# A transformer layer on one core: the order of jobs and values, transfers one by one, and layernorm roots by a power

## The chip, the core and the metric

The kernel runs on one core of one Trainium2 chip. A core has five engines with instruction streams of their own: TensorE (PE in the profile, its weight loads PEld), VectorE (DVE), ScalarE (ACT), GpSimd (POOL) and SyncE (SP), which issues nearly all transfers here. They share the on-chip memory SBUF; TensorE writes its products to PSUM, a second memory of 8 banks per partition, from which VectorE and ScalarE read them. Each engine works through its instructions in the order in which the program has them, and waits at semaphores for the others.

The metric is the device time of one execution in microseconds; lower is better.

## The reference

One pre-norm transformer layer, with a sequence of 2048, width 640, 32 heads of 20 and a hidden width of 1728. All inputs are bfloat16.

```python
def _A_ref(x, wqkv, wo):                      # B, S, D = 1, 2048, 640; H = 32; Dh = 20
    qkv = (x @ wqkv).reshape(B, S, 3, H, Dh).transpose(2, 0, 3, 1, 4)
    q, k, v = qkv[0], qkv[1], qkv[2]
    scores = jnp.einsum("bhqd,bhkd->bhqk", q, k) * (Dh ** -0.5)
    p = _softmax(scores, axis=-1)
    o = jnp.einsum("bhqk,bhkd->bhqd", p, v)
    return o.transpose(0, 2, 1, 3).reshape(B, S, D) @ wo
def _B_ref(x, w_gate, w_up, w_down):          # F = 1728
    g = jnp.einsum("bsd,df->bsf", x, w_gate)
    u = jnp.einsum("bsd,df->bsf", x, w_up)
    return jnp.einsum("bsf,fd->bsd", g * u, w_down)
h = x + _A_ref(_layernorm(x), wqkv, wo)       # _layernorm: (x - mean) / sqrt(var + 1e-5)
h2 = h + _B_ref(_layernorm(h), w_gate, w_up, w_down)
```

The softmax is over 32 x 2048 x 2048 scores, 134 million exponentials.

## The kernel before

**Tiling.** The heads are in 8 groups of 4; each head has a slot of 32 partitions, so four heads' scores or values run side by side in TensorE's array. Queries are in four blocks of 512 rows (b = 0 to 3), keys in 16 tiles of 128. A segment is one group's attention for one block (for the later blocks, of most groups, a half block of 256). All segments, one after the other, are cut into 683 score tiles of 1536 columns (three PSUM banks, two tiles in PSUM at a time).

**The main loop** runs over these tiles. `emit_S` issues a tile's scores (L533) and its exponential on ScalarE (L547), which writes bfloat16 into one of six buffers E. For some tiles the last 512 columns are left to VectorE, which makes the exponential of them with four instructions (L580 to L591): then ScalarE's tile has only 1024 columns. `x_takes` decides this by how much VectorE has to do and by how many such slices (tile xe) are still waiting to be used (`X_OUT`, 6). `emit_AV` takes the exponentials of finished tiles, two rounds of four heads at a time, and multiplies them with the values (L740); the extra column of ones in the values makes the softmax's sums. At a segment's end the accumulator is copied to SBUF (tile asb, L752); the sums go to DRAM and back over SP, are inverted on VectorE, broadcast by further transfers, and multiplied with asb some tiles later (`norm`).

**Jobs.** All other work of TensorE is in a queue of jobs, generators that yield one matmul (or one transposed tile) at a time: projections of queries, keys (L303) and values (L317), transposes of normalised rows (L283), the output projection (`job_out`, L978), the feed-forward's up and gate products (`job_glu`, L1065; with half blocks `glu_two`, L1083) and its second layer (`job_y`, L1129, 14 matmuls for half a row tile). Nearly all share one PSUM bank (tile mi): a job's result has to be evacuated by VectorE before the next job can begin. Where there is no job that fits, and TensorE's clock might fall, filler matmuls are issued (L496, L529).

**The planner.** The order on each engine is made while the program is built. The dictionary `at` holds estimated times: when TensorE, VectorE and ScalarE are done with what has been issued, when the bank mi is free (`at["mi"]`), when a score tile's slot is free. After a tile's scores and the values, `run_job(until)` issues pieces of jobs as long as they end, by the estimate, before the next scores have to be begun: `until` is the later of two times, the end of ScalarE's exponentials less 517 ns, and the moment at which the slot of the tile before the last is free. `spare` fills VectorE in the same way with layernorm steps and exponential slices. `later(n, fn)` calls a function n tiles further on.

**Layernorms.** Means and variances are made by VectorE (L201, L202). `rstd_steps` then rounds them to bfloat16 as the reference does, and makes the standard deviation on GpSimd with a shift of bits (L218), three Newton rounds of four instructions (L221 to L225) and a product (L232). At the earliest `ROOT_NS` (5000 ns) later, by the planner's clock, VectorE takes the reciprocal (L238) and normalises the rows. There are ten of these in the program's main part: three for the first layernorm (the first block's is made with ScalarE), seven for the second.

**Transfers.** When block 0's attention is finished, `add_tail` queues its output projection and feed-forward; its job `ready` asks for the rows of x, the first two pairs of up and gate weights (`load_w`) and all 14 tiles of the second-layer weights (`load_wd`, L956). When block 0's feed-forward is through, eight jobs `spill` copy the queries to DRAM (L935, L936), for a second pass that runs only if a sum is out of range; the freed SBUF then takes feed-forward weights for good (`load_res`). Other up and gate weights have two buffers each, and the next pair is asked for when a step begins (L1036).

**The end.** Behind the loop `last_tail` handles the last 256 rows: it issues the output projection (L1228, L1230, L1234), with the last group's normalisation in between (L670, L686), then statistics, ScalarE's root, and the normalised rows in halves on VectorE (L1257) and ScalarE (L1258). `fill()` issues all jobs that are left while these are made. Then come two tiles' transposes, the feed-forward, and the second layer with stores.

```python
            for f in range(2 * FP):
                p0 = max(0, (f + 1) * P - FF)
...
        for _ in range(2):
            emit_AV(i if i >= n_tiles else i - 2 if i >= LAG else i - 3)
...
            ran = run_job(max(at["exp"] - S_EXP - MARGIN, at["slot"][-2]))
...
        while cur["fresh"] or pe_free("F") + chunk() + SWITCH <= until:
            c = step()
            if c == FREE and cur["key"][0] not in ("spill", "load"):
```

Of the kernel before, what the change touches and what calls it, by code (L numbers as in the profile page):

```python
# [19 lines left out]
P = 128  # L20
# [40 lines left out]
RES_STEPS = 3  # L61
WO_NS, SUMS_NS, ROOT_NS, ROWS_NS = 1500, 6000, 5000, 5000
END_OF_TIME = 10 ** 9
WARM_LATE, NEXT_DVE = 0, 300
HOLD_AT, HOLD_NS = 5300, 450
AV_ROUNDS, X_LATE = 2, 0
FULL_IN, FULL_NS, ALL_NS = 2083, 300, 760
X_LEAST, X_OUT, X_SOON = 2, 6, 4
# [17 lines left out]
def kernel(  # L86
# [42 lines left out]
    huge = const.tile([P, 1], F32, name="huge")  # L129
    wo = [const.tile([P, D], BF16, name=f"wo{g}") for g in range(NG)]  # L130
# [52 lines left out]
    nc.gpsimd.memset(huge[:], 3.0e38)  # L183
    for c in range(KT):
        nc.vector.memset(wpad[c][:].rearrange("p m h e -> p (m h) e")[:, :, DH:SLOT], 0.0)
# [18 lines left out]
    def rstd_steps(mv, n, made, ve_=None):  # L204
        ve_ = ve_ or nc.vector
        mb = small.tile([P, n], BF16, name="mb")
        ve_.tensor_copy(mb[:], mv[:, :, 0])  # L207
# [7 lines left out]
        ve_.tensor_copy(v[:], ve[:])  # L215
        yield 1000 if ve_ is nc.vector else 50
        y = small.tile([P, n], F32, name="y")
        ve_.tensor_scalar(y[:].bitcast(I32), v[:].bitcast(I32), -0.5, float(0x5F3759DF), ALU.mult, ALU.add)  # L218
        t = small.tile([P, n], F32, name="nt")
        for k in range(3):  # L220
            ve_.tensor_tensor(t[:], y[:], y[:], ALU.mult)  # L221
            if ve_ is nc.gpsimd:
                ve_.tensor_tensor(t[:], t[:], v[:], ALU.mult)
                ve_.tensor_scalar(t[:], t[:], -0.5, 1.5, ALU.mult, ALU.add)
                ve_.tensor_tensor(y[:], t[:], y[:], ALU.mult)  # L225
            else:
                ve_.scalar_tensor_tensor(t[:], t[:], -0.5, v[:], ALU.mult, ALU.mult)
                ve_.scalar_tensor_tensor(y[:], t[:], 1.5, y[:], ALU.add, ALU.mult)
            if k != 2:
                yield (800, 600)[k] if ve_ is nc.vector else 50  # L230
        den = small.tile([P, n], BF16, name="den")
        ve_.tensor_tensor(den[:], v[:], y[:], ALU.mult)  # L232
# [5 lines left out]
        nc.vector.reciprocal(r[:], den[:])  # L238
        made.append((m32, r))
        yield 1000 if ve_ is nc.vector else 200  # L240
# [260 lines left out]
    def run_job(until):  # L501
# [9 lines left out]
        while cur["fresh"] or pe_free("F") + chunk() + SWITCH <= until:  # L511
            c = step()
            if c == FREE and cur["key"][0] not in ("spill", "load"):
                return run_job(until)
            if c in (None, NEXT, END, FREE):
                break
# [189 lines left out]

    def emit_AV(upto):
# [40 lines left out]
        if acc["left"] == 0:  # L748
            dve(605 if w == QB else 342, 0)
            if kind in ("copy", "only"):  # L750
                asb = parts[g] if kind == "copy" else nrm.tile([P, QB], F32, name="asb")
# [182 lines left out]
    def spill(g):  # L934
        nc.sync.dma_start(qsp[g][:, 0:QA], qa[g][:])  # L935
        nc.sync.dma_start(qsp[g][:, QA:S], qb[g][:])  # L936
# [14 lines left out]
    def load_wd():  # L951
        for f in range(2 * FP):
            p0 = max(0, (f + 1) * P - FF)
            if p0:
                nc.gpsimd.memset(late["Wd"][f][0:p0, :], 0.0)
            nc.sync.dma_start(late["Wd"][f][p0:P, :], B_w_down[f * P:f * P + P - p0, :])  # L956
# [120 lines left out]
    def glu_two(st, fp, c0, n):  # L1077
        u = late["s"].tile([P, QB], BF16, name="u")
        for k in range(2):
            ps = bank()  # L1080
            for f2 in range(2):
                for c in range(KT):
# [9 lines left out]
                    yield 216 * n // QB  # L1092
            yield NEXT
# [6 lines left out]
    def job_glu(st, ts, order=tuple(range(FP)), more=False):  # L1100
# [4 lines left out]
        for k, fp in enumerate(order):  # L1105
# [5 lines left out]
            if n <= HW and end["pool"] is None:  # L1111
                yield from glu_two(st, fp, c0, n)
# [52 lines left out]
    def add_tail(b, ts):  # L1165
        key = (b, ts[0])

        def ready():
            if key not in rows_in:
                rows(b, ts)  # L1170
            if b == 0:
                load_w(0, tail_st[b])
                load_w(1, tail_st[b])
                load_wd()
# [22 lines left out]
        if b == 0:  # L1197
            for g in range(NG):
                do(("spill", g), lambda g=g: spill(g))
# [18 lines left out]
    def last_tail():  # L1218
# [36 lines left out]
        for hf in range(2):  # L1255
            cs = slice(hf * HALF, (hf + 1) * HALF)
            nc.vector.tensor_scalar(ls[ta][:, cs], ps_h[ta, hf][:, 0:HALF], m32[:, 0:1], r[:, 0:1], ALU.subtract, ALU.mult)  # L1257
            nc.scalar.activation(ls[tb][:, cs], ps_h[tb, hf][:, 0:HALF], ACT.Identity, bias=mr[:, 1:2], scale=r[:, 1:2])  # L1258
        fill()
        run(job_T(ls[ta], st["ln2T"][:, :, ta * P:(ta + 1) * P], "dve", mip.tile([P, D], BF16, name="mi", tag="mi")))  # L1260
# [49 lines left out]
    while i < n_tiles or av_q:  # L1310
# [6 lines left out]
        if i == first_last:  # L1317
            for g in range(NG):
                ensure(("spill", g))
# [37 lines left out]
    def general():  # L1357
        st = new_st(None)
        st["res"] = {}
        with tc.For_i(0, S, P) as r0:  # L1360
# [3 lines left out]
            for g in range(NG):  # L1364
# [37 lines left out]
                oq = nrm.tile([P, HPG, SLOT], BF16, name="oq", tag="asb")  # L1402
# [41 lines left out]
```

## Time and profile before

| | |
|---|---|
| median of 3 runs | 916.38 us (915.68 to 917.12) |
| the profiled execution | 916.05 us, of which the span on the core is 914.0 us |
| granted TensorE clock, mean | 0.997 |
| score tiles on ScalarE | 515 of 1536 columns, 168 of 1024 columns |
| exponential slices on VectorE | 167 of 512 columns |
| first exponential begins, last one ends | 15.6 us, 869.9 us |
| transfers | 46.54 MB, mean 51 GB/s |

How to read the lines: the page begins with each engine's busy time, its share of the span and its number of instructions. A group's row names the line, the engine, the operation, the tile written and the tiles read, the shapes, the count, then the busy time in us and the mean of one in ns, and the idle time of the engine just before them with what ended it. A row of the timeline begins with its start and its length in us and ends in brackets with idle time before it and what ended that. A row of a table by stretches begins with the stretch in us from the span's start and its length. A row of the waits says who waited for whom, the us in total, the number of times, and the longest.

### The profile page before, as it was taken

How to read it: one execution, taken by the hardware profiler on the slowest of the kernel's cores; microseconds unless marked ns; L12 is line 12 of the kernel's file. 1: busy time of each engine (PE TensorE's matmuls, PEld its weight loads, DVE VectorE, ACT ScalarE, POOL GpSimd, SP SyncE). 2: the span in 40 equal slices, each digit the busy share in tenths (PEclk: the TensorE clock that was granted, in tenths of full speed). 3: DMA queues.
4: the chain of work that ended last, by engine and by line, in shares of the span. 5: the costliest groups of instructions: out<-in, count | busy, mean ns of one | idle time of the engine just before them, and what ended most of it. 6: DMA issues, size and time to landing. Idle time of an engine off the chain costs nothing.

```text
span 914.0 us, 20094 instructions
## 1 busy us (share of the span) xinstructions
PE 817.5 (89%) x8035; PEld 346.8 (38%) x8115; DVE 702.1 (77%) x1310; ACT 866.2 (95%) x719; POOL 57.4 (6%) x255
## 2 busy tenths in 40 slices
PE   8788999889989899899897888999998999998897
PEld 5233333222223222233232333434434445444575
DVE  8664349899999899899998999798998784542243
ACT  6999999999999999999999999999999999999931
POOL 4210000000001200000003000020001000010000
PEclk9999999999999999999999999999999999999999
DMA  6000011011025022212410022021411211201310
GB/s 195 17 14 1 1 27 27 14 24 37 4 61 149 13 71 72 64 49 90 160 28 14 20 70 68 19 54 49 117 51 42 73 28 51 57 15 50 80 44 18
DMA packets 74203, 46.54 MB, mean 51 GB/s; under 512 B 20380, under 2 KB 70440, under 8 KB 74104
## 3 DMA queue, kind: packets, MB, share of 16 engines
q1 hardware_dynamic: 74104, 45.20, 18.0%
q8 instruction: 65, 1.06, 0.5%
q14 instruction: 34, 0.28, 0.1%
HBM read 37.88 MB, written 7.30 MB: 49 GB/s over the span
## 4 chain that ended last, share of the span: by engine, by line
ACT 67%; issue 17%; PE 10%; DVE 4%; DMA 1%; POOL 1%; SPq 0%; ACTq 0%
ACT E L547 67%; PE sc L533 2%; PE f L1065 2%; PE f L1129 2%; PE acc L740 1%; DVE st L201 1%; PE mi L303 1%; PE mi L978 0%; PE f L1230 0%; PE mi L496 0%; DMA wu<-in_B_w_up_dram 0%; PE mi L317 0%; PE mi L1083 0%; DVE kT L310 0%; DVE vx L270 0%
## 5 line engine op out<-in xcount | busy, mean ns | idle before, releaser
L547 ACT ACTIVATE E<-sc 128x1536 bf16<-128x1536 f32 (+1 forms) x683 | 848.7, 1417 | 6.2 <-PE sc L533 5.9
L533 PE MATMUL sc<-qa,kT 32*128 32x512 bf16 (+1 forms) x1920 | 203.2, 340 | 28.6 <-ACT E L547 16.9
L533 PEld LDWEIGHTS <-kT 32*128 32x128 bf16 x2816 | 84.1, 91 | 244.6 <-issue 206.1
L740 PE MATMUL acc<-E,vx 128*32 128x256 bf16 (+1 forms) x2592 | 170.3, 326 | 1.7 <-DVE vx L270 1.2
L580 DVE TENSOR_SCALAR xv<-sc 128x512 f32<-128x512 f32 x167 | 115.0, 689 | 30.2 <-PE sc L533 26.5
L585 DVE SCALAR_TENSOR_TENSOR xe<-xt,xv 128x512 int16<-128x512 f32 x167 | 113.3, 682 | 1.0
L591 DVE SCALAR_TENSOR_TENSOR xt<-xt,xv 128x512 f32<-128x512 f32 x167 | 112.3, 681 | 0.5
L590 DVE SCALAR_TENSOR_TENSOR xt<-xv 128x512 f32<-128x512 uint16 x167 | 112.0, 683 | 0.3
L303 PE MATMUL mi<-lnT,wp 128*128 128x512 bf16 x279 | 83.3, 381 | 11.7 <-DVE qa L310 5.5
L740 PEld LDWEIGHTS <-vx 128*32 128x32 bf16 x2816 | 55.8, 95 | 66.4 <-issue 63.8
L533 PE MATMUL sc<-qb,kT 32*128 32x256 bf16 (+1 forms) x896 | 68.2, 288 | 8.1 <-ACT E L547 5.3
L1129 PE MATMUL mi<-wd,hh 128*128 128x320 bf16 x336 | 58.2, 301 | 1.6 <-DVE xr L1133 1.6
L740 PE MATMUL acc<-xe,vx 128*32 128x512 bf16 (+1 forms) x224 | 50.6, 332 | 0.0
L1129 PEld LDWEIGHTS <-hh 128*128 128x128 bf16 x448 | 38.7, 97 | 30.6 <-issue 18.7
L303 PEld LDWEIGHTS <-wp 128*128 128x128 bf16 x310 | 25.0, 97 | 55.9 <-issue 44.3
L310 DVE TENSOR_SCALAR kT<-mi,one_row 128x512 bf16<-128x512 f32 x30 | 22.5, 750 | 28.1 <-PE mi L303 24.7
L1065 PE MATMUL mi<-ln2T,wg 128*128 128x512 bf16 x128 | 38.0, 382 | 5.8 <-DVE u L270 5.2
L496 PE MATMUL mi<-kT,ident 128*128 128x512 bf16 x116 | 37.8, 386 | 5.5 <-DVE ln2T L270 1.0
L978 PE MATMUL mi<-wo,on 128*128 128x320 bf16 x224 | 40.5, 301 | 2.2 <-DVE xr L982 2.0
L1065 PE MATMUL mi<-ln2T,wu 128*128 128x512 bf16 x128 | 37.3, 382 | 4.3 <-DVE hh L1073 3.5
L1083 PE MATMUL mi<-ln2T,qa 128*128 128x256 bf16 x240 | 34.6, 274 | 4.1 <-DVE hh L1091 3.0
L207 POOL CAST mb<-mv 128x2 bf16<-128x2 f32 (+1 forms) x10 | 2.3, 231 | 528.6 <-DVE mv L202 410.9
(143 smaller groups left out, 645.0 us busy)
## 6 DMA issues: line engine op xcount, KB each, us to landing
wu<-in_B_w_up_dram SPq DMA_DIRECT2D x23, 320.0 KB
wg<-in_B_w_gate_dram SPq DMA_DIRECT2D x23, 320.0 KB
bc<-scr SPq DMA_DIRECT2D x80, 64.0 KB
qsp<-qa SPq DMA_DIRECT2D x8, 384.0 KB
xr<-in_A_x_dram SPq DMA_DIRECT2D x16, 160.0 KB
bc<-scr SPq DMA_DIRECT2D x76, 32.0 KB
out_dram<-xr SPq DMA_DIRECT2D x14, 160.0 KB
wd<-in_B_w_down_dram SPq DMA_DIRECT2D x13, 160.0 KB
```

The source lines that it names most:

```text
L303: nc.tensor.matmul(ps[:], lhsT=wslice(m, g, c), rhs=lnT[:, c, ch * QB:(ch + 1) * QB], start=(c == 0), stop=(c == KT - 1))
L496: nc.tensor.matmul(ps[:], lhsT=ident[:], rhs=kT[0][:, 0:BANK], start=True, stop=True)
L533: nc.tensor.matmul(sc[:, o:o + w], lhsT=kT[g][SLOT * j:SLOT * (j + 1), kt * P:(kt + 1) * P], rhs=q_of(g, b, c0, w)[SLOT * j:SLOT * (j + 1) ...
L547: exps = nc.scalar.activation(e[:, 0:n_act], sc[:, 0:n_act], ACT.Exp, bias=EXP_BIAS, scale=SM_SCALE)
L580: took = nc.vector.tensor_scalar(v[:], ps, X_SCALE, X_BASE, ALU.mult, ALU.max)
L585: nc.vector.scalar_tensor_tensor(e[:], t[:], X_R, v[:], ALU.mult, ALU.add)
L590: lambda: nc.vector.scalar_tensor_tensor(t[:], u, X_P, u, ALU.add, ALU.mult),
L591: lambda: nc.vector.scalar_tensor_tensor(t[:], t[:], X_Q, u, ALU.add, ALU.mult),
L740: nc.tensor.matmul(acc["t"][SLOT * j:SLOT * (j + 1), 0:w], lhsT=vx[kt][:, VS * h:VS * h + SLOT], rhs=e, start=(acc["n"][j] == 0), stop=(ac ...
L978: nc.tensor.matmul(ps[:, 0:HALF], lhsT=on[g][:, t * P:(t + 1) * P], rhs=wo[g][:, cs], start=(g == 0), stop=(g == NG - 1))
L1065: nc.tensor.matmul(ps[:, 0:n], lhsT=st["w", fp][k][:, c, f_cols(fp, f2)], rhs=st["ln2T"][:, c, c0:c0 + n], start=(c == 0), stop=(c == KT - 1))
L1129: nc.tensor.matmul(ps[:, 0:HALF], lhsT=st["hh"][f // 2][:, f % 2, t * P:(t + 1) * P], rhs=late["Wd"][f][:, cs], start=(f == 0), stop=(f == ...
```

## The change

Line numbers of the diff aside, these are all its parts. Constants: `X_OUT` goes from 6 to 5 buffers, the copies asb from 2 to 3, and a tile `half` holds 0.5.

```diff
+RES_STEPS, WD_AT, WD_STEPS, SPILL_AT = 3, 10, 2, 60
+LN_NS = 3300
-X_LEAST, X_OUT, X_SOON = 2, 6, 4
+X_LEAST, X_OUT, X_SOON = 2, 5, 4
+    half = const.tile([P, TPB], F32, name="half")
+    nc.gpsimd.memset(half[:], 0.5)
```

The root: shift, three rounds and product are replaced with one power on GpSimd, and the pauses between the rounds go.

```diff
         ve_.tensor_copy(v[:], ve[:])
-        yield 1000 if ve_ is nc.vector else 50
-        y = small.tile([P, n], F32, name="y")
-        ve_.tensor_scalar(y[:].bitcast(I32), v[:].bitcast(I32), -0.5, float(0x5F3759DF), ALU.mult, ALU.add)
-        t = small.tile([P, n], F32, name="nt")
-        for k in range(3):
...
         den = small.tile([P, n], BF16, name="den")
-        ve_.tensor_tensor(den[:], v[:], y[:], ALU.mult)
+        ve_.tensor_tensor(den[:], v[:], half[:, 0:n], ALU.pow)
```

Jobs before values: from tile 10 on, ahead of the values, a job that is under way gets the time that remains until the next scores are due, less the estimate for the values that are ready (`av_ns` returns 0 where `emit_AV` would issue none).

```diff
+    def av_ns(upto):
+        if not av_q or acc["seg"] not in (None, av_q[0][1]):
+            return 0
+        s = av_q[0][1]
+        if acc["seg"] is None and at["pe"] < at["acc"] and now["i"] < acc["from"] and min(u[0] for u in av_q) > now["i"] - E_BUFS:
+            return 0
+        w = PASS[segs[s][0]][2]
+        most, rows = AV_ROUNDS * QB // w, [0] * HPG
+        for u in av_q:
+            if u[0] > upto or u[1] != s:
+                break
+            rows[u[3]] = min(rows[u[3]] + 1, most)
+        left = acc["left"] if acc["seg"] == s else END_OF_TIME
+        if sum(rows) < min(most * HPG, left) and min(u[0] for u in av_q) > upto - E_BUFS + 3:
+            return 0
+        return SWITCH + -(-sum(rows) // HPG) * (w * 5 // 12 + 4)
+
+    def job_ahead(upto):
+        ns = av_ns(upto)
+        if not ns:
+            return
+        until = max(at["exp"] - S_EXP - MARGIN, at["slot"][-2]) - ns
+        if not cur["fresh"]:
+            run_job(until)
...
+        if LAG <= i < n_tiles:
+            job_ahead(i - 2)
         for _ in range(2):
             emit_AV(i if i >= n_tiles else i - 2 if i >= LAG else i - 3)
```

Transfers: the first up and gate weights come 3 and 7 tiles after the job `ready`, the second-layer tiles one by one from 10 tiles after it, and the spills one by one from 60 tiles after block 0's tail has been queued.

```diff
-    def load_wd():
-        for f in range(2 * FP):
...
+    def load_wd(f):
+        p0 = max(0, (f + 1) * P - FF)
...
             if b == 0:
-                load_w(0, tail_st[b])
-                load_w(1, tail_st[b])
-                load_wd()
+                for fp in range(2):
+                    later(4 * fp + 3, lambda fp=fp: load_w(fp, tail_st[b]))
+                for f in range(2 * FP):
+                    later(WD_AT + WD_STEPS * f, lambda f=f: load_wd(f))
...
             for g in range(NG):
-                do(("spill", g), lambda g=g: spill(g))
+                later(SPILL_AT + 4 * g, lambda g=g: spill(g))
```

An up-weight is asked for, by half blocks, when the up products that used its buffer have been issued, and no longer together with the gate weight:

```diff
+    def load_up(fp, st):
+        if ("w", fp) not in st and fp not in late["next"] and fp not in st["res"]:
+            st["up", fp] = [w_tile(B_w_up, fp, late["w"].tile([P, KT * FPW], BF16, name="wu"))]
...
-            st["w", fp] = [w_tile(src, fp, late["w"].tile([P, KT * FPW], BF16, name=nm))
-                           for nm, src in (("wu", B_w_up), ("wg", B_w_gate))]
+            two = st["w", fp] = st.pop(("up", fp), [])
+            for nm, src in (("wu", B_w_up), ("wg", B_w_gate))[len(two):]:
+                two.append(w_tile(src, fp, late["w"].tile([P, KT * FPW], BF16, name=nm)))
...
-    def glu_two(st, fp, c0, n):
+    def glu_two(st, fp, c0, n, up_done):
...
+            if k == 0:
+                up_done()
             yield NEXT
...
-                yield from glu_two(st, fp, c0, n)
+                far = order[k + 2] if order[1] not in st["res"] and k + 2 < FP else None
+                yield from glu_two(st, fp, c0, n, lambda: far is not None and load_up(far, st))
```

The end: when `fill()` has issued less than 3300 ns of work by the planner's clock, matmuls into an unused bank follow it.

```diff
+        begun = at["pe"]
         fill()
+        warm_ps = bank()
+        for _ in range(int((LN_NS - (at["pe"] - begun)) / 216)):
+            nc.tensor.matmul(warm_ps[:], lhsT=ident[:], rhs=kT[0][:, 0:BANK], start=True, stop=True)
```

More of the change, by code (lines that the diff above doesn't have):

```diff
@@ L60 @@
 TOL, LEAST, MARGIN = 200, 216, 20
-RES_STEPS = 3
+RES_STEPS, WD_AT, WD_STEPS, SPILL_AT = 3, 10, 2, 60
 WO_NS, SUMS_NS, ROOT_NS, ROWS_NS = 1500, 6000, 5000, 5000
@@ L512, in run_job @@
             c = step()
-            if c == FREE and cur["key"][0] not in ("spill", "load"):
+            if c == FREE and cur["key"][0] != "load":
                 return run_job(until)
@@ L750, in emit_AV @@
             if kind in ("copy", "only"):
-                asb = parts[g] if kind == "copy" else nrm.tile([P, QB], F32, name="asb")
+                asb = parts[g] if kind == "copy" else nrm.tile([P, QB], F32, name="asb", bufs=3)
                 nc.vector.tensor_copy(asb[:, 0:w], acc["t"][:, 0:w])
@@ L934, in spill @@
     def spill(g):
+        if ("spill", g) in done:
+            return
+        done.add(("spill", g))
         nc.sync.dma_start(qsp[g][:, 0:QA], qa[g][:])
@@ L949, in open_late @@
         late["Wd"] = [late["wd"].tile([P, D], BF16, name=f"wd{f}") for f in range(2 * FP)]
-    def load_wd():
-        for f in range(2 * FP):
[L953 to L956, printed above, removed]
+    def load_wd(f):
+        p0 = max(0, (f + 1) * P - FF)
+        if p0:
+            nc.gpsimd.memset(late["Wd"][f][0:p0, :], 0.0)
+        nc.sync.dma_start(late["Wd"][f][p0:P, :], B_w_down[f * P:f * P + P - p0, :])
     def new_st(rows_of):
@@ L1318 @@
             for g in range(NG):
-                ensure(("spill", g))
+                spill(g)
             load_res()
@@ L1401, in general @@
                 nc.vector.reciprocal(ri[:], ov[:, :, DH:VS])
-                oq = nrm.tile([P, HPG, SLOT], BF16, name="oq", tag="asb")
+                oq = nrm.tile([P, HPG, SLOT], BF16, name="oq", tag="asb", bufs=3)
                 nc.vector.memset(oq[:], 0.0)
```

10 lines of the change are left out of this document (removed).

## The prediction

> **What bounds the kernel now.** I read the engines' busy times first, then the chain of work that ended last, then the exponential's line (L547) by stretches, and last the timeline of the end.
>
> ```profile
> PE 817.5 (89%) x8035; PEld 346.8 (38%) x8115; DVE 702.1 (77%) x1310; ACT 866.2 (95%) x719; POOL 57.4 (6%) x255
> ACT 67%; issue 17%; PE 10%; DVE 4%; DMA 1%; POOL 1%; SPq 0%; ACTq 0%
> 15.60:60.00 44.40, 40.56 (x30) 1.00 0.10 31
> 60.00:500.00 440.00, 439.75 (x359) 1.00 0.17 47
> 500.00:520.00 20.00, 19.51 (x17) 0.91 0.06 16
> 520.00:870.00 350.00, 348.90 (x280) 1.00 0.21 54
> 870.00:914.00 44.00, 0.00 (x0) 0.97 0.11 32
> ```
>
> The last five rows are L547 alone: stretch, ACT's busy time, granted clock, DMA share, GB/s. From 60 to 870 us ACT computes exponentials for 808.2 of 810 us, so work that other engines save there is worth nothing; only fewer columns on ACT, or its 1.8 us of idle, can shorten it. Two other parts differ: 15.6 to 60 us, where ACT waits about 4 us for scores, and the 44 us after the last exponential, in which TensorE and its dependences set the end.
>
> **The change part by part.** The planner runs while the program is built, so I compared the instruction lists of the two built programs.
>
> (1) *Exponentials.* VectorE takes 172 slices of 512 columns in place of 167; ACT has 510 wide and 173 narrow tiles in place of 515 and 168.
>
> ```profile
> L547 ACT ACTIVATE E<-sc 128x1536 bf16<-128x1536 f32 x486 | 677.6, 1523 | 1.5 <-PE sc L533 1.4
> L547 ACT ACTIVATE E<-sc 128x1024 bf16<-128x1024 f32 x168 | 178.2, 1100 | 0.5 <-PE sc L533 0.5
> L590 DVE SCALAR_TENSOR_TENSOR xt<-xv 128x512 f32<-128x512 uint16 x167 | 112.0, 683 | 0.3
> ```
>
> A narrow tile is 1523 - 1100 = 423 ns shorter, and five are 2.1 us. VectorE pays 5 x 4 x 0.68 = 13.7 us, spread over 800 us in which it is 77% busy; five slices uncovered would cost 2.7 us each. Bounds -2.1 to 0; I take -2.1, because ACT is never idle in that stretch.
>
> (2) *The roots.* Per layernorm the shift, three rounds of four and the product, 14 GpSimd instructions, become one power.
>
> ```profile
> 21.77 0.19 POOL L207 CAST mb<-mv 128x4 bf16<-128x4 f32 x1 [3.80 <-DVE mv L202]
> 22.71 0.19 POOL L215 CAST v<-ve 128x4 f32<-128x4 bf16 x1
> 26.60 0.20 POOL L232 TENSOR_TENSOR den<-v,y 128x4 bf16<-128x4 f32 x1
> 28.13 0.17 DVE L238 RECIPROCAL rstd<-den 128x4 f32<-128x4 bf16 x1
> 485.46 0.17 DVE L238 RECIPROCAL rstd<-den 128x2 f32<-128x2 bf16 x1 [1.07 <-POOL den L232]
> 489.60 1.45 ACT L547 ACTIVATE E<-sc 128x1536 bf16<-128x1536 f32 x1 [0.22 <-PE sc L533]
> ```
>
> The trace has no power. Its nearest row is the two-input product at 0.20 us; the far bound is what it replaces, 26.80 - 22.90 = 3.9 us. Anything between is hidden by VectorE's other work until the reciprocal at 28.13, and I take 0.2 to 0.3. From 28.13 - 22.90 = 5.2 us on, VectorE would wait in order, with its evacuations and exponentials behind the reciprocal. The gain is the late root at 485 us: VectorE waited 1.07 us, and ACT 0.22 us for the scores behind it. So -0.2 (bounds -0.2 to 0).
>
> (3) *Transfers.* Second-layer weights go from one burst of 14 to one each two score tiles, spills from 16 in a row to two each four tiles and some 60 tiles earlier, and an up-weight is asked for as soon as the matmuls that held its buffer are issued.
>
> ```profile
> L956 SPq DMA_DIRECT2D wd<-in_B_w_down_dram x14: 327/419/1409, 273.4 to 282.0; - x14
> 431.64 0.43 SPq L935 DMA_DIRECT2D qsp<-qa  x1
> 441.92 0.46 SPq L936 DMA_DIRECT2D qsp<-qb  x1
> 756.23 0.42 SPq L1036 DMA_DIRECT2D wu<-in_B_w_up_dram  x1
> 759.73 1.27 PE L1083 MATMUL mi<-ln2T,wu 128*128 128x256 bf16 x10 [1.03 <-DMA wu<-in_B_w_up_dram]
> 761.44 2.88 ACT L547 ACTIVATE E<-sc 128x1536 bf16<-128x1536 f32 x2 [0.84 <-PE sc L533]
> ```
>
> The bursts hold SP for some 9 and 11 us, but ACT lost 0.25 us in the whole of 60 to 500 us, so breaking them up is worth 0: sums and broadcasts, queued behind them, had slack. The weight asked for at 756.23 came 1.03 us late and cost ACT 0.84 us; asked for one half-step earlier, it is in time. An earlier request makes SP wait for the up matmuls (1.3 us), with the sums' transfers behind it; normalisation waits many tiles for those. I take -0.8 (bounds -0.8 to 0).
>
> (4) *Jobs ahead of values.* In 63 of 289 value rounds the rest of a half-done projection or feed-forward step (none before) now precedes the values. It frees its PSUM bank earlier, because VectorE evacuates while TensorE multiplies values. The last feed-forward step ends at score tile 671, not in the last one (682), so 42 of the 56 second-layer matmuls that stood in the fill behind the loop move into tiles 677 to 682. TensorE also has 18 more filler matmuls (L496) in the loop, i.e. more idle time in the plan. The trace can't price a displaced value round: 0 if the plan's deadline (unchanged) holds, and at the worst each of the 63 waits as TensorE does now for a bank:
>
> ```profile
> PE mi L1065 <- DVE u L270: 5.2, 12, 0.7
> ACT E L547 <- PE sc L533: 5.9, 9, 1.1
> ```
>
> that is 5.2/12 = 0.43 us each, 27 us in all. Of 683 exponentials only 9 waited for scores, most before 60 us; the plan is nearest to that row, so I take 0. Between 15.6 and 60 us the lists differ little (a handful of pieces change places): 0, bounds -4 (all of the waits there) to +2 (half as much again).
>
> (5) *The end.* Here the rows are of the execution before:
>
> ```profile
> 869.95 0.40 PE L740 MATMUL acc<-E,vx 128*32 128x256 bf16 x6 [0.52 <-ACT E L547]
> 875.98 7.83 PE L1129 MATMUL f<-wd,hh 128*128 128x320 bf16 x56
> 878.28 1.12 DVE L1257 TENSOR_SCALAR ln<-f,m,rstd 128x320 bf16<-128x320 f32 x2
> 878.44 1.13 ACT L1258 ACTIVATE ln<-f,mr,rstd 128x320 bf16<-128x320 f32 x2 [0.48 <-DVE mr L1253]
> 883.65 0.44 PE L283 MATMUL mi<-ident,ln 128*128 128x128 bf16 x5
> 883.93 0.44 PE L283 MATMUL acc<-ident,ln 128*128 128x128 bf16 x5
> 885.15 5.07 PE L1065 MATMUL f<-ln2T,qa 128*128 128x256 bf16 x45 [0.78 <-ACT ln2T L267]
> ```
>
> The last normalisation's rows are ready at 878.28 + 1.12 = 879.40 and 879.57, yet TensorE is in 56 second-layer matmuls until 883.65: 4.2 us are lost. Now 14 stay there, and two warming matmuls; 7.83/56 = 0.14 us each makes 2.0 us, well before the rows are ready. But the new list also has nine of the moved matmuls between the last values and the output projection, on the path: 9 x 0.14 = 1.25 us later for all that follows. The rows are then ready at 880.65 and 880.82. From the first transposes to the feed-forward took 885.15 - 883.65 = 1.50 us, so it begins near 882.2: 885.15 - 882.2 = 3.0 us earlier. From there on nothing differs. If all 56 remained on the path it would be 0, and without the nine -4.2; I take -3.0.
>
> *Sum:* -2.1 - 0.2 - 0.8 + 0 - 3.0 = -6.1 us on the profiled execution's 916.05 us (span 914.0), hence 909.95. That execution lies 0.33 us under the median of 916.38, so I predict 910.2.
>
> **Weighed against the skill.** The clock first:
>
> ```profile
> 501.50:505.00 3.50, 2.13 (x40) 0.76 (x36) 2.97 (x5) 3.50 (x5) 2.41 (x9) 1.00 0.00 0
> 505.00:508.50 3.50, 3.17 (x36) 1.00 (x31) 3.38 (x7) 3.50 (x4) 0.00 (x0) 0.54 0.05 7
> L533 PE MATMUL sc<-qa,kT 32*128 32x256 bf16 x18 | 1.2, 271 | 1.4 <-ACT E L547 1.4
> L740 PE MATMUL acc<-E,vx 128*32 128x256 bf16 x20 | 0.9, 275 | 0.0
> L496 PE MATMUL mi<-kT,ident 128*128 128x512 bf16 x2 | 0.6, 385 | 0.0
> ```
>
> At 505 us the granted clock fell to 0.54 for one such stretch, after one (its groups are the last three rows) with TensorE 2.13 us busy, all but 0.6 us of it on matmuls that use a quarter of the array. Behind the new fill (2.0 us from 877.2, two warming matmuls at the 0.6 us of the last row, so to about 879.8) TensorE has only ten transposes until 882.2, i.e. a 2.4 us lull. The Trainium skill ("TensorE: Matmul & The Clock Gate", Part 1, "What's actually happening", and Part 4) says that an idle window of about 3.4 us halves the clock, and that transposes don't count as busy. By that rule a 2.4 us lull fills no window, and the sum stays; by the row, where a busier stretch sufficed, it would not.
>
> **Rivals.**
> - *The lull halves the clock.* For: the row above; against: full-array matmuls frame the lull. One stretch of 3.5 us at half speed loses about 1.7 us: 911.9.
> - *Displaced values stall ACT (slower).* Where a job's rest takes longer than planned, values, the next scores and ACT are all late, and E's six buffers empty later. For: 15.6 to 60 us, where the same planner lost ACT some 4 us in 30 tiles; against: the 1.8 us in 653 tiles later. At 0.05 us for each of 63 places: 913.4. From 6.1/63 = 0.10 us on the gain is gone, and at 0.15 us it is 919.7.
> - *The power is slow.* If one took 8 us, each of ten roots would come up to 8 - 5.2 = 2.8 us late; with half of that reaching ACT, 14 us more: 924. Against: no GpSimd row of this trace, however wide, is above 1 us.
> - *The change doesn't do what it says at the end:* the moved matmuls don't fit into tiles 677 to 682 (42 x 0.14 = 5.9 us in 8 us of exponentials, beside scores and values). Then ACT waits up to 3 us there and the end gains nothing net: 913.2.
> - *The early waits vanish too:* 910.2 - 4 = 906.2.
>
> **How the numbers follow.** The forecast has 0.56 (its own range 908 to 912), the lull 0.12, the values rival 0.17 (0.09 of it at or above 916, most of that slower), the slow power 0.02, the end rival 0.08, the early waits 0.05. From 906.5 to 915.5 all but about 0.13 lies inside. A median of this kernel tells apart some 0.2%, 1.8 us: faster (under 914.5) 0.86, same 0.05, slower (over 918.2) 0.09.
>
> **What would show it.** (1) L547 in 510 wide and 173 narrow tiles, with ACT's idle time after 60 us still at or below 2 us. (2) A power of under 1 us, and no wait of the reciprocal for it. (3) No wait for an up-weight, and none new for a sum or a broadcast. (4) The last feed-forward step of the loop done well before its last score tile. (5) Nine second-layer matmuls ahead of the output projection, 14 behind it, and 885.15 - 869.95 = 15.2 us from the last values to the feed-forward become about 12.2, at granted clock 1.00. The prediction is wrong if ACT's idle time grows by more than 3 us, if a reciprocal waits for its power, or if the clock falls behind the fill.

## The result, and the profile after

Over 20 runs each, the changed kernel takes 913.0 us (911.92 to 915.77) and the one before 916.65 us (915.61 to 917.76): 3.65 us less, with a ratio of 0.9965 (95% interval 0.9959 to 0.9972). The forecast was 6.1 us less, 910.2 us (908 to 912). The sign was right, and a little more than half of the size came.

The changed kernel's page, and the exponential (now L535) by stretches: stretch, ACT's busy time in it, granted clock, DMA share, GB/s.

```profile
span 911.1 us, 20122 instructions
PE 834.6 (92%) x8138; PEld 344.3 (38%) x8138; DVE 714.1 (78%) x1330; ACT 864.6 (95%) x719; POOL 32.7 (4%) x126
ACT 55%; PE 24%; issue 13%; DVE 7%; DMA 1%; SPq 0%; ACTq 0%; DVEq 0%
```

```profile
60.00:500.00 440.00, 438.84 (x359) 1.00 0.17 47
500.00:520.00 20.00, 20.00 (x18) 1.00 0.06 17
520.00:870.00 350.00, 347.83 (x280) 1.00 0.21 55
870.00:911.10 41.10, 0.00 (x0) 0.97 0.11 31
```

ScalarE's exponentials are 1.5 us shorter there (806.7 us instead of 808.2), but its idle time between 60 and 870 us is 1.5 us longer (3.3 instead of 1.8), so the loop ends where it ended before, at 870 us. All of the span's 2.9 us come from the end, 41.1 us instead of 44.1. The chain of waits says the same: ACT's share of it falls from 67% to 55%, and TensorE's rises from 10% to 24%. Who kept ScalarE waiting is seen in its waits (in total, times, longest):

```profile
ACT E L535 <- PE sc L521: 3.8, 5, 1.1
ACT E L535 <- PE acc L753: 2.8, 5, 1.2
```

The first line lies before 60 us; after it no exponential waits for scores any more (before there were three such waits, 1.55 us). The second line is new. It isn't the scores that are late there, but values: an exponential can't be written, because the buffer E that it is to take has not yet been read. The five are 0.39, 0.67, 0.45, 1.17 and 0.17 us long, at 323, 401, 555, 569 and 791 us. The largest, in ScalarE's, TensorE's and VectorE's timelines:

```profile
569.54 2.37 ACT L535 ACTIVATE E<-sc 128x1536 bf16<-128x1536 f32 x2 [1.17 <-PE acc L753]
```

```profile
567.16 0.39 PE L1085 MATMUL mi<-ln2T,wu 128*128 128x512 bf16 x1
567.48 0.28 PE L753 MATMUL acc<-xe,vx 128*32 128x256 bf16 x1
...
567.81 0.40 PE L521 MATMUL sc<-qa,kT 32*128 32x256 bf16 x6
568.14 0.39 PE L753 MATMUL acc<-xe,vx 128*32 128x256 bf16 x2
569.05 0.62 PE L753 MATMUL acc<-E,vx 128*32 128x256 bf16 x16 [0.52 <-DVE asb L765]
```

```profile
567.29 0.69 DVE L568 TENSOR_SCALAR xv<-sc 128x512 f32<-128x512 f32 x1
567.89 0.68 DVE L258 CAST u<-mi 128x512 bf16<-128x512 f32 x1
568.57 0.42 DVE L765 COPY asb<-acc 128x256 f32<-128x256 f32 x1
```

This is a segment's end. The last up matmul (567.16) now goes ahead of the segment's last values, and its evacuation (567.89) ahead of the accumulator's copy (568.57). The next segment's values (569.05), which would free the buffer, wait for that copy, and they stand in TensorE's list behind the scores of the very tile whose exponential needs the buffer. ScalarE waits 1.17 us.

### The profile page after: what moved, and what is told of

The parts are those of the page before. It is cut to its first block, busy times and chain, and to the rows that moved or that the text cites. A ratio compares the mean times of both kernels' runs of the same rounds, so it can differ in the third digit from the quotient of the medians.

```text
span 911.1 us, 20122 instructions
## 1 busy us (share of the span) xinstructions
PE 834.6 (92%) x8138; PEld 344.3 (38%) x8138; DVE 714.1 (78%) x1330; ACT 864.6 (95%) x719; POOL 32.7 (4%) x126
## 3 DMA queue, kind: packets, MB, share of 16 engines
q8 instruction: 65, 1.06, 0.5%
## 4 chain that ended last, share of the span: by engine, by line
ACT 55%; PE 24%; issue 13%; DVE 7%; DMA 1%; SPq 0%; ACTq 0%; DVEq 0%
ACT E L535 55%; PE sc L521 5%; PE acc L753 4%; PE mi L1085 3%; PE mi L1103 3%; PE f L1085 2%; PE mi L1152 1%; PE mi L484 1%; DVE st L204 1%; PE f L1152 1%; DVE hh L1093 1%; DVE u L1108 1%; PE mi L291 0%; DVE xt L579 0%; PE f L1254 0%
## 5 line engine op out<-in xcount | busy, mean ns | idle before, releaser
L535 ACT ACTIVATE E<-sc 128x1536 bf16<-128x1536 f32 (+1 forms) x683 | 847.1, 1412 | 7.3 <-PE sc L521 3.8
L568 DVE TENSOR_SCALAR xv<-sc 128x512 f32<-128x512 f32 x172 | 118.6, 689 | 35.7 <-PE sc L521 32.4
L573 DVE SCALAR_TENSOR_TENSOR xe<-xt,xv 128x512 int16<-128x512 f32 x172 | 115.9, 680 | 0.6
L579 DVE SCALAR_TENSOR_TENSOR xt<-xt,xv 128x512 f32<-128x512 f32 x172 | 115.3, 682 | 0.5
L578 DVE SCALAR_TENSOR_TENSOR xt<-xv 128x512 f32<-128x512 uint16 x172 | 115.1, 683 | 0.2
L1152 PE MATMUL mi<-wd,hh 128*128 128x320 bf16 x378 | 65.2, 301 | 0.3 <-DVE xr L1156 0.2
L753 PE MATMUL acc<-xe,vx 128*32 128x256 bf16 (+1 forms) x232 | 52.9, 329 | 0.0
L484 PE MATMUL mi<-kT,ident 128*128 128x512 bf16 x164 | 49.5, 383 | 2.9 <-DVE ln2T L258 1.2
L1085 PE MATMUL mi<-ln2T,wu 128*128 128x512 bf16 x140 | 40.4, 381 | 6.2 <-DVE hh L1093 5.9
L1085 PE MATMUL mi<-ln2T,wg 128*128 128x512 bf16 x140 | 40.8, 383 | 2.1 <-DVE u L258 1.9
L305 PE MATMUL mi<-wv,lnT 128*128 128x320 bf16 x160 | 28.5, 300 | 4.7 <-DVE vx L258 2.7
```

What stands on the lines that cost most here:

```text
L484: nc.tensor.matmul(ps[:], lhsT=ident[:], rhs=kT[0][:, 0:BANK], start=True, stop=True)
L535: exps = nc.scalar.activation(e[:, 0:n_act], sc[:, 0:n_act], ACT.Exp, bias=EXP_BIAS, scale=SM_SCALE)
L568: took = nc.vector.tensor_scalar(v[:], ps, X_SCALE, X_BASE, ALU.mult, ALU.max)
L573: nc.vector.scalar_tensor_tensor(e[:], t[:], X_R, v[:], ALU.mult, ALU.add)
L578: lambda: nc.vector.scalar_tensor_tensor(t[:], u, X_P, u, ALU.add, ALU.mult),
L579: lambda: nc.vector.scalar_tensor_tensor(t[:], t[:], X_Q, u, ALU.add, ALU.mult),
```

## The experiments

All times are medians, beside the runs of the kernel before on the same chip.

**1. The change without jobs ahead of values.**

```diff
-        if LAG <= i < n_tiles:
-            job_ahead(i - 2)
```

> The changed kernel without jobs ahead of values; every other part is kept. By its instruction list it has 167 slices on VectorE and 56 matmuls in the fill, as before. Theory A (jobs ahead of values bring the shorter end and the five slices, and also the five new waits of the exponential for values, 2.8 us): no wait of the exponential for values, and the time of before less the late weight and the late root, 916.65 - 1.0 = 915.6 (914.8 to 916.4). Rival B (the waits come from the fewer exponential buffers, the third copy or the pauses that went from the layernorm): 2 to 3 us of such waits stay, and with the gains gone the time is 917.5 to 919.

914.62 us against 916.36 (ratio 0.9988, 0.9978 to 0.9999). No exponential waits for values; in this run's waits ScalarE's only ones for the exponential are

```profile
ACT E L535 <- PE sc L521: 4.4, 7, 1.1
```

of which all but 0.2 us lie before 60 us. So what is left of the change (the power, the transfers, and the pauses and buffers that go with them) brings 1.1 us by the ratio and 1.7 us by the medians, about the 1.0 us that power and transfers were forecast to, and the waits for values come with the jobs ahead. But with only 1.6 us between this and the whole change, the jobs ahead bring far less than the 5.1 us (exponentials 2.1, end 3.0) put down to them.

**2. Jobs ahead of values alone, on the kernel before.** The edit is `av_ns`, `job_ahead` and its call.

> The kernel before with jobs ahead of values alone. Its list has 174 slices on VectorE, 14 matmuls in the fill and nine ahead of the output projection. Theory A: seven slices save 7 x 0.42 = 3.0 us, the end 3.0 us, and waits for values of 2 to 4 us come in: 912.6 to 914.6. Rival B: no such wait, about 910.7. The late weight (0.84 us) stays in both.

918.51 us against 916.36 (1.0027, 1.001 to 1.0044): some 0.3% slower. Both theories missed. VectorE's and ScalarE's waits in this run show what was not thought of:

```profile
DVE rstd L238 <- POOL den L232: 6.2, 4, 3.4
DVE ri L647 <- DMA sums_all<-sums: 2.4, 1, 2.4
ACT E L547 <- PE sc L533: 8.4, 12, 1.6
ACT E L547 <- PE acc L765: 1.2, 2, 0.7
```

In the new order VectorE comes to three of the late reciprocals 4.3 to 5.4 us after the layernorm's first step on GpSimd (L207), where it never came sooner than 6.4 us in the kernel before; the Newton roots are late four times instead of twice. And a segment's sums are late because their two transfers (the second asked for at 275.9 us) now stand behind the burst of second-layer weights; in the kernel before the second was asked for at 268.5 us, and the burst began at 273.4 us. The transfers that cost nothing in the old order cost something in this one. In this profile the granted clock was also halved just behind the fill (the next rows: TensorE's busy time, the others', then the clock), and its end was 1.6 us longer than the changed kernel's:

```profile
881.00:885.00 4.00, 2.54 (x23) 1.56 (x21) 3.40 (x12) 1.64 (x4) 0.00 (x0) 1.00 0.00 0
885.00:889.00 4.00, 3.56 (x19) 2.58 (x20) 0.42 (x1) 2.35 (x7) 0.00 (x0) 0.60 0.74 205
```

**3. The power alone.** The kernel before with the power, and the pauses of the layernorm kept.

```diff
-        y = small.tile([P, n], F32, name="y")
...
-        ve_.tensor_tensor(den[:], v[:], y[:], ALU.mult)
+        ve_.tensor_tensor(den[:], v[:], half[:, 0:n], ALU.pow)
```

> The kernel before with the power in place of the shift, rounds and product, and with the pauses kept, so that every engine but GpSimd has the list of before. Expected by the prediction: the two late roots (1.07 and 0.91 us on VectorE) go, ACT gains 0.2 us, 916.4 (916.0 to 916.8). Rival C (the power, measured at 0.73 to 1.06 us, disturbs VectorE while it runs): 917 or more.

915.84 us against 916.36 (0.9994, 0.9982 to 1.0006): no difference that these runs can tell from none, as expected of 0.2 us; nothing of rival C.

**4. The transfers alone.** The kernel before with `load_wd(f)`, `spill` and the first weights by `later`, and `load_up`.

> The kernel before with the transfers of the change alone (weights and spills one by one, up-weight early). Same counts of slices and fill as before. Expected: the up-weight's 1.03 us wait goes, ACT gains 0.8 us, 915.8 (915.4 to 916.3). Rival D (the spread transfers hold SP when sums are due): new waits for sums or broadcasts, 917 or more.

916.33 us against 916.36 (1.0000, 0.9991 to 1.0009). The 0.8 us didn't show in the median, though in the profile the wait of 759 us is gone; the interval of some 0.8 us either way doesn't rule it out. Rival D's waits aren't there either.

**5. Seven buffers E.**

```diff
-    ep = pool("ep", E_BUFS)
+    ep = pool("ep", E_BUFS + 1)
```

This version leaves out the range check of the sums and the third copy asb, for room.

> The changed kernel with seven buffers E in SBUF in place of six, while the planner still plans for six, so that TensorE's and ScalarE's lists are those of the changed kernel. For its room the third copy asb is given up, and the sums' range check is left out (the check reads a constant, the second pass is never run). Theory A (ScalarE waits for buffers E that the values have not yet read, since the round at a segment's end is displaced): the five waits of the exponential for values, 2.8 us, go, and the time is 913.0 - 2.8 = 910.2 (909.4 to 911.2). Rival E (what ends late there is TensorE as a whole, so the scores would be late in place of the buffer): new waits for scores of the same size, 912.5 to 913.5.

911.36 us against 916.5 (0.9939, 0.9927 to 0.9952), five runs from 910.17 to 913.2. No exponential waits for values. The waits for scores in the profile, and the one at 569 us, where 0.66 of the 1.17 us stays as a wait for scores:

```profile
ACT E L536 <- PE sc L522: 6.5, 9, 1.1
569.59 2.37 ACT L536 ACTIVATE E<-sc 128x1024 bf16<-128x1024 f32 x2 [0.66 <-PE sc L522]
```

The profiled execution was the slowest of the five, with the clock halved twice in it (0.62 between 50 and 54 us, 0.57 between 858 and 862 us): of the 2.7 us by which its waits for scores are longer than the changed kernel's, 2.1 us stand in or right behind these two stretches, and 0.66 us at 569 us. So this profile shows that the waits for values go, but not the gain; that is in the median, 0.2 us above theory A's range and 1.1 us below rival E's. Mostly theory A, with a part of rival E at that place; experiment 12 is the clearer case.

**6. Two copies asb in place of three.**

> The changed kernel with two copies asb, as before, and the same lists on every engine. Theory A: the third copy is not what the segment's end waits for: 913.0 (912.4 to 913.8), the same five waits. Rival F (a copy to a buffer that is still to be multiplied holds VectorE and so the next segment's values): more than five waits for values, 914.5 or more.

912.99 us against 916.5 (0.9966, 0.9955 to 0.9978), with the same five waits of the same lengths. The third copy plays no part.

**7. The half tile under way is finished in the fill.**

```diff
-    while ("loadB",) not in done or not cur["fresh"]:
+    while ("loadB",) not in done:
```

> The changed kernel in which the second-layer half that is under way when the loop ends is finished in the fill, so that its nine matmuls are not ahead of the output projection; by the planner's clock no warming matmul is then needed. The prediction's term of 1.25 us: rows of the last normalisation are ready 1.25 us earlier and the fill of 23 x 0.136 = 3.1 us still ends before: 913.0 - 1.25 = 911.75 (911.3 to 912.4). Rival: 23 matmuls end with the rows and the transposes come no earlier, 912.5 to 913.2; and if the lull behind the fill halves the clock, 1.7 us more.

912.56 us against 916.5 (0.9956, 0.9943 to 0.9969), 0.4 less than the changed kernel: the full 1.25 us doesn't come, and the medians can't tell 0.4 us from nothing. The profile can say where it goes. TensorE and VectorE at that place:

```profile
870.34 0.40 PE L753 MATMUL acc<-E,vx 128*32 128x256 bf16 x6 [0.19 <-ACT E L535]
...
876.37 1.39 PE L1152 MATMUL mi<-wd,hh 128*128 128x320 bf16 x9
877.60 2.06 PE L1152 MATMUL f<-wd,hh 128*128 128x320 bf16 x14
880.24 0.44 PE L271 MATMUL mi<-ident,ln 128*128 128x128 bf16 x5 [0.58 <-DVE xr L1156]
...
881.73 2.45 PE L1085 MATMUL f<-ln2T,qa 128*128 128x256 bf16 x21 [0.78 <-ACT ln2T L255]
```

```profile
878.66 1.12 DVE L1281 TENSOR_SCALAR ln<-f,m,rstd 128x320 bf16<-128x320 f32 x2
879.70 0.48 DVE L1156 TENSOR_TENSOR xr<-mi,xr 128x320 bf16<-128x320 f32 x1
```

The rows are ready 9.4 us after the last values began (879.78 - 870.34), instead of 10.7 (880.72 - 870.05 in the changed kernel), so 1.2 us of the nine matmuls are off the path. But their result lies in the bank mi, which the first transposes need; VectorE evacuates it behind the rows, at 879.70, and the transposes wait 0.58 us for it. From last values to feed-forward it is 11.4 us instead of 12.1, 0.7 us less.

**8. No warming matmuls.**

> The changed kernel without the two warming matmuls behind the fill, all else equal. In the run with jobs ahead alone, which had none either, the granted clock was halved for 3.4 us right there, and that run's end was 1.6 us longer than the changed kernel's. If the two matmuls prevent it: the clock falls in this run too, 913.0 + 1.6 = 914.6 in most runs. If the stretches of the gate fall by chance: it falls in some of the runs only, median 913.0 to 913.8.

913.15 us against 916.5 (0.9964, 0.9951 to 0.9977), with the clock at full speed behind the fill in the profile. So the two matmuls aren't what the changed kernel's end depends on. With none, the clock fell there in the profile of experiment 2, but not in this one, nor in those of experiments 9 and 10, which have experiment 2's order on TensorE; how often it does was not measured.

**9. Jobs ahead and the power**, and **10. jobs ahead and the transfers**, each on the kernel before: experiment 2 with one part more, and exactly its lists on TensorE, ScalarE and VectorE.

> Jobs ahead of values and the power together on the kernel before (pauses of the layernorm kept): TensorE's, ScalarE's and VectorE's lists are exactly those of the run with jobs ahead alone (918.5 us), only GpSimd's differs. There VectorE waited four times, 6.2 us, for late roots, and ScalarE 2.0 us for scores right behind the longest (3.4 us). Theory G (jobs ahead alone is slow because it makes the Newton roots late, and the power is what it needs): no wait of a reciprocal, ScalarE's waits about 310 us gone, 918.5 - 2.0 to 2.5 = 916.0 to 916.5. Rival H (what was slow there is the order itself): 918 or more with no late root.

> Jobs ahead of values and the transfers of the change together on the kernel before, again with the three engines' lists of the run with jobs ahead alone; only SP's differs. There VectorE waited 2.4 us for sums behind the burst of second-layer weights, and ScalarE 1.6 us at 280 us. Theory G': that wait goes, 918.5 - 1.6 to 2.0 = 916.5 to 917.0, while the late roots stay. Rival H: 918 or more.

(One reading in the first of these is to be put right: the 2.0 us that ScalarE lost about 310 us in experiment 2 stand behind the wait of 1.62 us for the root at 308 us; the longest, 3.39 us, ended at 513.6 us.)

915.51 us against 916.58 (0.9994, 0.9981 to 1.0008) and 914.81 us (0.9981, 0.9971 to 0.9991). With the power no reciprocal waits any more, but the sums are 3.6 us late behind the burst, and ScalarE waits 2.8 us for the scores behind them:

```profile
278.74 0.25 DVE L638 RECIPROCAL ri<-sums_all 128x16 f32<-128x16 f32 x1 [3.62 <-DMA sums_all<-sums]
```

```profile
281.65 2.37 ACT L538 ACTIVATE E<-sc 128x1024 bf16<-128x1024 f32 x2 [2.80 <-PE sc L524]
```

With the transfers it is the other way round: no wait for sums, and the four late roots stay (6.2 us in total, as in experiment 2).

The waits go as theory G says for both, and rival H doesn't hold. In the old order the power was worth 0.5 us and the transfers 0.0 us, neither told apart from nothing; with jobs ahead the medians fall by 3.0 us (918.5 to 915.5) and 3.7 us (918.5 to 914.8), more than theory G gave them. Not all of that is shown to be the waits: in the profiles the stretch from the first exponential to the last is 2.0 and 1.2 us shorter than experiment 2's (855.3 and 856.1 us against 857.3), and the rest of the spans' difference is an earlier first exponential and experiment 2's longer end, with its halved clock.

**11. Values one tile earlier when buffers run out.**

```diff
-        if acc["seg"] is None and ... and min(u[0] for u in av_q) > now["i"] - E_BUFS:
+        if acc["seg"] is None and ... and min(u[0] for u in av_q) > now["i"] - E_BUFS + 1:
...
-            if not av_q or min(u[0] for u in av_q) > i - E_BUFS + 1:
+            if not av_q or min(u[0] for u in av_q) > i - E_BUFS + 2:
```

(The first line stands in `av_ns` and, in the same form, in `emit_AV`.)

> The changed kernel with three thresholds of the planner moved by one tile (two where a new segment's values may wait, one for the second round of values), so that values are issued one tile earlier when buffers E run out. In the changed kernel's list the values of tile i - 6, whose buffer tile i's exponential takes, stand behind the scores of tile i at ten places (three in the kernel before); here only at one, in the first ten tiles. It has 175 slices on VectorE (172) and 42 matmuls in the fill (14), none ahead of the output projection. Theory A: the waits for values go (-2.8 us), three slices save 1.3 us, the end is about 1 us longer: 913.0 - 3.1 = 909.9 (909.0 to 911.2). Rival: values that are forced early make TensorE wait in order for the accumulator's copy, and the scores behind it are late: 912 or more, with new waits for scores.

918.62 us against 916.58 (1.0026, 1.0017 to 1.0034): the rival. ScalarE's waits for values go, and longer ones for scores come in their place. Its waits and TensorE's for the accumulator's copy (0.5 us, once, in the changed kernel), and one of them in TensorE's and ScalarE's timelines:

```profile
ACT E L535 <- PE sc L521: 11.1, 14, 1.3
PE acc L753 <- DVE asb L765: 5.8, 10, 1.1
```

```profile
727.66 0.62 PE L753 MATMUL acc<-E,vx 128*32 128x256 bf16 x14 [0.52 <-DVE asb L765]
728.21 0.40 PE L521 MATMUL sc<-qb,kT 32*128 32x256 bf16 x6
```

```profile
728.73 3.71 ACT L535 ACTIVATE E<-sc 128x1536 bf16<-128x1536 f32 x3 [0.89 <-PE sc L521]
```

The values wait for the accumulator's copy as before, but now the scores are queued behind them. What is late at a segment's end is the copy; which engine pays for it is a matter of order. The waits for scores grow by 7.3 us, and the end, with 42 matmuls in the fill, is 1.8 us longer than the changed kernel's (42.9 us).

**12. Seven buffers E, with nothing left out.** The sums of one half are kept at a time and their extremes taken once in between, which frees the room; two copies asb; the half tile of experiment 7.

```diff
-    sums_all = const.tile([P, N_SUMS], F32, name="sums_all")
+    sums_all = const.tile([P, 256], F32, name="sums_all")
...
+        if col["n"] + n > 256:
+            nc.vector.tensor_reduce(ext[:, 2:3], bits, axis=AX.X, op=ALU.min)
+            nc.vector.tensor_reduce(ext[:, 3:4], bits, axis=AX.X, op=ALU.max)
+            col["n"] = 0
```

> A version that might beat both, with nothing left out: the changed kernel with seven buffers E, two copies asb, the half tile under way at the loop's end finished in the fill, and the room for the seventh buffer from keeping the sums of one half at a time (their extremes are taken once in the middle, two more VectorE instructions of some 0.35 us in the loop). TensorE's and ScalarE's lists are those of the run with the half tile in the fill (912.56). Theory A: the waits for values go as in the run with seven buffers, -1.6 to -2.8 us: 910.0 to 911.2. Rival: the two reductions come where VectorE is late already, 911.5 to 912.5.

909.55 us against 916.52 (0.9927, 0.9914 to 0.9941), five runs from 909.54 to 910.44: better than both kernels, and 3.0 us under experiment 7, whose lists on TensorE and ScalarE it has. ScalarE's exponentials between 60 and 867 us:

```profile
60.00:867.00 807.00, 805.78 (x653) 1.00 0.19 50
```

1.2 us of idle time are left in 807 us.

## Why the prediction was right in sign and wrong in size

**(1) Exponentials: right.** 510 wide and 173 narrow tiles, and ACT's busy time after 60 us 1.5 us shorter, where 2.1 was forecast.

**(2) The roots: right as a term, and too small as a part.** A power took 0.73 to 1.06 us, near the low end of the bounds, not 0.2 to 0.3. No reciprocal waited:

```profile
L220 POOL TENSOR_TENSOR den<-v,half x10: 727/930/1056, 23.6 to 810.4; 128x2 bf16<-128x2 f32 x7, 128x4 bf16<-128x4 f32 x3
```

That is far from the 5.2 us from which it would have been late, so the rival of a slow power is out. What the prediction didn't see is that roots and transfers were costed in the old order. In the new one the old roots are late by 6.2 us in total instead of 2.0 (experiments 2 and 10), and with the power none is (experiment 9).

**(3) Transfers: the waits right, the gain alone not seen.** The late weight is gone, but the 0.8 us that it was to bring isn't in the median of experiment 4 (0.0 us, some 0.8 us either way), which also gives the broken-up bursts no worth in the old order, as said. With jobs ahead the sums would have been 2.4 us late behind the burst, and the median falls by 3.7 us with the transfers (experiment 10).

**(4) Jobs ahead of values: this step failed.** The displaced values were priced at 0, "the plan is nearest to that row", the row of waits for scores. They cost 2.8 us, in five waits of ScalarE for buffers E. The row was the wrong one: the planner's deadline, on which the zero rested, is for the scores, and it was kept: after 60 us no exponential waits for scores. For a buffer E the planner has no time, only counts of tiles (the thresholds that experiment 11 moves). ScalarE's idle time after 60 us, which was to stay at or below 2 us, is 3.3 us. With the ring of seven those waits go and the time falls by 1.6 us (experiment 5) and, beside experiment 7, 3.0 us (experiment 12). The mechanism was among the rivals ("E's six buffers empty later"), but with 0.05 us for each of 63 places it was priced as an even spread and not at the segments' ends; that its 913.4 us lies near the measured 913.0 is luck. It could have been read before the run, from the list: at ten places, against three in the kernel before and none with seven buffers, the values of tile i - 6 stand behind the scores of tile i, whose exponential takes that buffer. Five of the ten (tiles 240, 304, 432, 443 and 624, counted from 0) became the five waits. By the same count there are three in experiment 1, with no such wait, and six in experiment 2, with two; with `X_OUT` left at 6 the changed kernel has the same ten. Why some of the places cost nothing was not looked into.

**(5) The end: right.** Nine second-layer matmuls ahead of the output projection, 14 in the fill, and the feed-forward begins at 882.18, forecast at 882.2:

```profile
870.05 0.40 PE L753 MATMUL acc<-E,vx 128*32 128x256 bf16 x6 [0.19 <-ACT E L535]
870.38 1.40 PE L1152 MATMUL mi<-wd,hh 128*128 128x320 bf16 x9
...
877.30 2.06 PE L1152 MATMUL f<-wd,hh 128*128 128x320 bf16 x14
879.21 0.59 PE L1287 MATMUL f<-kT,ident 128*128 128x512 bf16 x2
...
882.18 8.02 PE L1085 MATMUL f<-ln2T,qa 128*128 128x256 bf16 x72 [0.78 <-ACT ln2T L255]
```

12.1 us from the last values, where 12.2 was forecast. The nine matmuls cost 1.25 us where they stand, but moving them to the fill gains only 0.7 us in the profile, since most of the rest comes back as a wait for the bank mi (experiment 7). The moved matmuls fitted into the loop's last tiles, so that rival is out as well.

**The sum, by the profiles.** Forecast -6.1 us, measured 914.0 - 911.1 = 2.9 us less in span. Of the 3.2 us that are missing, 2.8 us are the waits for values. Two more parts are 0.6 us by which the first exponential came later (16.2 us, not 15.6; between 15.5 and 16.2 in the profiles of this study), and 0.6 us of exponentials, which became 1.5 us shorter and not 2.1. Against them, the waits for scores fell by 2.1 us (5.9 to 3.8), where (2) and (3) forecast 1.0; 0.5 us of that stood at 509.6 us, right behind the halved clock in the profile of the kernel before, and is luck of that execution. That makes 2.9 us; the rest is in waits of 0.2 us or less. By the medians the changed kernel lies 2.8 us above the forecast of 910.2 us (909.95 + 0.33 is nearer to 910.3).

**The lull and the skill.** In the changed kernel the clock stayed at 1.00 behind the fill:

```profile
880.00:884.00 4.00, 2.73 (x27) 2.30 (x28) 1.85 (x5) 3.18 (x8) 0.00 (x0) 1.00 0.41 108
```

The Trainium skill ("TensorE: Matmul & The Clock Gate", Part 1, "What's actually happening") lets the clock fall after an idle window of about 3.4 us; with a lull of 2.4 us here that agrees. Experiments 2, 8, 9 and 10, without the warming matmuls, all have a lull of 2.8 us there. In the first of them the clock fell behind it (at 885.8 us, with TensorE 1.5 us busy in the 3.4 us before, most of that on the ten transposes), and in the other three it stayed at 1.00. So this lull halves the clock in some executions and not in others. And the two falls of experiment 5 (the last section) came with TensorE 2.5 and 2.8 us busy in the 3.4 us before, so an idle window is not what it takes, and the measurement decides: the lull was a risk, and the fall was absent in the profile of the changed kernel.

## What to carry to other kernels

Before costing a new order at zero because the plan's deadlines hold, list every resource that the reordered work releases, and count in the instruction list how often a release now stands behind the work that needs it; here a deadline for scores was kept while a buffer ring without a deadline ran dry. A part that is worth nothing in the old order (faster roots, thinner transfers) can be what makes a tighter order work, so its worth is measured within the new order too. And where a release is late by less than one tile, one more buffer can be cheaper than forcing the order: here 911.4 us (experiment 5) against 918.6 (experiment 11).

## What the runs showed of the hardware that was not expected

- The granted clock was halved for 3.4 us at a time while TensorE was far from idle: after 4 us with TensorE 3.08 us busy, and after 4 us with 3.40 us busy, in the profile of experiment 5. (At half the clock, the 0.05 and 0.38 of 4 us that the first two rows lack come to 3.4 us, and so do the 0.43 of 4 us of the last.)

```profile
46.00:50.00 4.00, 3.08 (x24) 1.00 (x22) 1.54 (x3) 2.87 (x3) 0.00 (x0) 0.95 0.31 113
50.00:54.00 4.00, 3.96 (x22) 1.26 (x16) 2.73 (x7) 3.23 (x3) 0.00 (x0) 0.62 0.02 4
854.00:858.00 4.00, 3.40 (x45) 1.85 (x43) 1.00 (x4) 4.00 (x4) 0.00 (x0) 1.00 0.85 223
858.00:862.00 4.00, 4.00 (x37) 1.59 (x36) 0.76 (x2) 3.68 (x4) 0.00 (x0) 0.57 0.78 206
```

  ACT lost some 0.8 and 0.3 us in the second and fourth of these, and waited 1.0 us more for scores just behind the last, at 863.5 us. The mean granted clock differs from run to run of one kernel: in the changed kernel's 20 runs, 911.9 to 915.8 us, it goes from 1.000 down to 0.995, and the four runs at 0.996 or less are among the five slowest. That these falls are what made them slow was not shown.
- A power of two values per partition took 835 ns on GpSimd, four times a product (195 ns at its median), and still replaced 14 instructions that took 3.8 to 6.2 us.
